# Seven half-size products for the last matrix product of a retention and gated-MLP kernel

## Chip, cores and metric

The kernel runs on one core of a Trainium2 chip. The metric is device time in microseconds of one execution; below, the median of three runs. TensorE does the matrix products, DVE (VectorE), ACT (ScalarE) and POOL (GpSimd) work element by element, and all data moves by DMA issued from SP's queue.

## What is computed

```python
scores = scale * q @ k.T * gamma[h] ** (i - j)   # causal, 8 heads of 64, 576 positions, 8 batches
x = (scores @ v)  ->  (batch, 576, 512)
h = relu(x @ w_in)                               # 512 -> 1024
u, v = h[..., :512], h[..., 512:]
v_n = (v - mean(v)) / sqrt(var(v) + 1e-6)
v_s = w_spatial @ v_n + b_spatial                # over the 576 positions
out = (u * v_s) @ w_out                          # 512 -> 512
```

## The kernel before

Retention is computed in four chunks of 128 positions and a tail of 64, with a state carried from chunk to chunk, on 64x64 matmuls. The rest are matmuls of 128 rows by 128 columns of weights with 256, 288 or 512 moving columns. Each fp32 operand is kept as two parts, an upper one in the matmul's number format (`hi`, an ACT copy that rounds) and the rest (`lo`, a subtraction); a product of two such operands is three matmuls, hi*hi, hi*lo and lo*hi (`mm3`). So before an operand can be used, ACT has to round it and DVE or POOL to subtract.

The order of every instruction on every engine is written out by hand in two tables. `ORDER` covers the weights and batches 0 and 1, and the start of batch 2. `STEADY` is run six times, for batches a = 2 to 7, with b = a + 1 and c = a + 2 for what is already started of the next ones; names with a batch past 7 are left out. A name stands for a chain (a generator), and each time that it occurs its next step is issued. Each engine and the DMA queue runs its instructions in the order in which the tables issue them, and waits for its data. `BANKS` names, in the same order, the one of four PSUM banks that each larger product uses. The names that matter here:

- `d.b.c`, `T.b`: loads of chunk c and of the tail of batch b. `k`, `q`: scaling of a chunk's keys and queries.
- `g` scores and mask, `p` state update, `b` the burst of products of a chunk and its evacuation (steps: carried products, `turned`, carried products, values, evacuation), `t` the tail's scores and mask, `e` its evacuation.
- `R`, `K`: for batches 2 to 7, the input x (kept in fp32 in `x32`) is cut in quarters; `R` splits three quarters as they are (`plain_quarter`), and `K` forms four differences of quarters and splits them (`summed_quarter`): a subtraction, an ACT cast, a subtraction. The letters at the end of a name (`p`, `v`) choose POOL or DVE for the first and last of them.
- `W.b.kind.m.i`: product i of seven (Strassen's scheme, in Winograd's form) of x and w_in, kind 0 for the v half and kind 1 for the u half, for output half m; each is six matmuls and then one to two additions into `u`. `A.s.step` makes the weights' combinations for it.
- `v`: relu and normalization. `X.b.t.db`: `w_spatial` times v_n, then the gate with u, then the split of the result into hi and lo in a `slot` (`g_chain`).
- `F.b.t.mb`: the product of the gated result and w_out, 12 matmuls for each of eight output blocks, an ACT copy to a tile `o0` to `o3`, and its DMA out (`f_chain`).

There are two `slot` tiles of two parts by four 128-row blocks by 576 columns. For batches 2 to 7 the seven right factors of x lie in seven quarters of the two slots, and the split gated product takes all of slot 1; so `K`, which writes quarters of slot 1, can only follow `F` of the batch before.

Of the kernel before, what the change touches and what calls it, by code (L numbers as in the profile page):

```python
# [10 lines left out]
F32 = mybir.dt.float32  # L11
# [35 lines left out]
    p.0.1.vv v.0.0 p.0.1.vv k.0.2.p b.0.1 w.0.0.vp b.0.1 q.0.2.p w.0.0.vp g.0.2 b.0.1 w.0.1.pp w.0.1.pp b.0.1
    p.0.2.pp T.0 p.0.1.vv d.0.3 w.0.2.pp p.0.2.pp v.0.0 b.0.1 v.0.0 g.0.2 w.0.1.pp p.0.2.pp w.0.1.pp b.0.2 p.0.2.pp
    b.0.2 c.t w.0.2.pp p.0.2.pp v.0.1 v.0.1 t.0.p t.0.p w.0.1.pp k.0.3.v b.0.2 b.0.2 d.1.0 w.0.2.pp q.0.3.p g.0.3
    t.0.p p.0.3.pp v.0.1 p.0.3.pp v.0.0 v.0.1 p.0.3.pp b.0.2 b.0.2 v.0.2 g.0.3 S d.1.0 p.0.3.pp d.1.1 b.0.3 m  # L50
    w.0.0.vp b.0.3 d.1.1 v.0.1 g.1.0 b.0.3 b.0.3 k.1.0.p w.0.2.pp S v.0.2 v.0.2 d.1.0 v.0.0 D.2.1 q.1.0.p s.0.p
    g.1.0 e.0.p v.0.0 S v.0.1 p.1.0.vv S e.0.p w.0.2.pp v.0.1 b.0.3 v.0.0 e.0.p S v.0.2 v.0.4 v.0.0 v.0.4 k.1.1.p
    p.1.0.vv v.0.2 d.1.2 s.2.p v.0.4 v.0.1 b.0.3 v.0.0 q.1.1.p v.0.1 w.0.0.vp s.1.v v.0.2 v.0.4 d.1.1 p.1.0.vv v.0.3
    s.2.p v.0.3 v.0.1 s.0.p v.0.2 w.0.2.pp s.4.p v.0.3 U.1 v.0.3 v.0.4 p.1.0.vv s.5.v d.1.2 b.1.0 T.1 U.1 s.3.v
    g.1.1 p.1.1.pp s.1.v v.0.2 v.0.4 p.1.0.vv b.1.0 s.4.p b.1.0 s.5.v k.1.2.p s.3.v v.0.2 v.0.2 b.1.0 p.1.1.pp D.0.3
    v.0.4 U.0 b.1.0 p.1.1.pp b.1.0 v.0.3 v.0.4 v.1.0 w.0.2.pp v.0.3 d.1.2 U.0 g.1.1 w.0.1.pp w.0.1.pp v.1.0 v.1.0
# [868 lines left out]
```

## Time and profile before

| | |
|---|---|
| median of three runs | 528.0 us (527.73 to 528.03) |
| the profiled execution | 528.6 us, span 526.7 us |
| TensorE busy | 499.3 us (95%), 7376 matmuls |
| DVE, POOL, ACT busy | 353.3 us (67%), 236.6 us (45%), 222.0 us (42%) |
| granted TensorE clock | 0.996 of full speed |
| one pass of STEADY | 61.12 us |

The span runs from the first to the last instruction. In the lists of instructions, each line has the start in us, the duration in us, the engine, the operation, "out<-in" by the program's tile names (numbers left out: `m` is a PSUM bank of the larger products, `r` a PSUM tile of retention, `x` is `x32`), the shape, the count, and in square brackets the idle time of the engine before it with what ended it. Rows of windows give start and end, the length, then busy time and count of PE, PEld (weight loads), DVE, ACT and POOL, then granted clock, share of the DMA engines in use and GB/s. Rows of groups give busy time, mean ns of one, and the idle time before them by releaser. All lines bear the number 155, that of the helper which records every operation, so the tiles tell them apart.

### The profile page before, as it was taken

To read this page: it belongs to the slowest core of one execution; us is meant where nothing else is said; L and a number is where in the kernel's file an instruction comes from. 1 tells how busy PE (TensorE), PEld (TensorE's weight loads), DVE (VectorE), ACT (ScalarE), POOL (GpSimd) and SP (SyncE) were. 2 spreads that over 40 slices of the span, in tenths; PEclk is the share of its full clock that TensorE was granted. 3 is DMA by queue.
4 is the path that set the end of the run, shared out by engine and by line. 5 is a ranking of instruction groups with operands and counts; after the bars stand their busy time and mean duration, and the time that the engine had idled before them with its cause. 6 is when DMAs were issued, how large, how long until landed. Compare 5 with 4: busy or idle time off the path is not lost.

```text
span 526.7 us, 17043 instructions
## 1 busy us (share of the span) xinstructions
PE 499.3 (95%) x7376; PEld 475.8 (90%) x7376; DVE 353.3 (67%) x803; ACT 222.0 (42%) x502; POOL 236.6 (45%) x216
## 2 busy tenths in 40 slices
PE   0789999999998999999999999999999999999897
PEld 0668998799998999999999999999999999998896
DVE  4998888961536884579654995569745895538640
ACT  4347535562152452444344451445434452444422
POOL 2887769411156720667027740557216750444000
PEclk9999999999998999999999999999999999999999
DMA  8995342403315430163202650155201600020002
GB/s 289 410 321 187 116 157 82 123 18 101 113 59 170 144 105 2 46 197 126 78 2 94 182 168 4 42 157 160 87 2 52 221 11 2 1 91 1 0 1 91
DMA packets 29948, 55.53 MB, mean 105 GB/s; under 512 B 3249, under 2 KB 15793, under 8 KB 29618
## 3 DMA queue, kind: packets, MB, share of 16 engines
q1 hardware_dynamic: 29874, 54.45, 31.4%
q8 instruction: 58, 0.95, 0.7%
q14 instruction: 16, 0.13, 0.1%
HBM read 45.00 MB, written 9.44 MB: 103 GB/s over the span
## 4 chain that ended last, share of the span: by engine, by line
PE 80%; DVE 9%; POOL 3%; issue 3%; DMA 2%; ACT 2%; SPq 0%; ACTq 0%; POOLq 0%; DVEq 0%
PE m L155 69%; PE r L155 11%; DVE u L155 3%; DMA lent_slot<-in_w_in 1%; POOL x L155 1%; DVE sm L155 1%; DMA kn<-in_qkv 1%; POOL u L155 1%; DVE m L155 1%; DVE s L155 1%; DVE vn L155 1%; DVE slot L155 1%; SPq L155 0%; ACT vt L155 0%; DVE dec L155 0%
## 5 line engine op out<-in xcount | busy, mean ns | idle before, releaser
L155 PE MATMUL m<-wsp,vn 128*128 128x288 f32 x768 | 113.5, 297 | 0.4 <-DVE vt L155 0.3
L155 PEld LDWEIGHTS m<-wsp,vn 128*128 128x128 f32 x768 | 105.2, 188 | 2.0 <-DVE vt L155 1.3
L155 PE MATMUL m<-slot,wout 128*128 128x288 f32 x768 | 104.1, 294 | 0.2 <-DVE f L155 0.2
L155 PEld LDWEIGHTS m<-slot,wout 128*128 128x128 f32 x768 | 102.3, 188 | 0.7 <-issue 0.6
L155 PE MATMUL m<-slot,win 128*128 128x288 f32 x480 | 74.2, 299 | 1.8 <-ACT u L155 1.0
L155 DVE TENSOR_TENSOR u<-m,u 128x256 f32<-128x256 f32 (+1 forms) x144 | 59.0, 431 | 24.5 <-ACT u L155 16.5
L155 PEld LDWEIGHTS m<-slot,win 128*128 128x128 f32 x480 | 66.7, 188 | 5.9 <-ACT u L155 2.6
L155 PE MATMUL m<-win,slot 128*128 128x256 f32 (+1 forms) x312 | 56.5, 325 | 2.7 <-issue 1.8
L155 POOL TENSOR_TENSOR x<-x 128x576 f32<-128x576 f32 (+1 forms) x28 | 42.7, 1524 | 21.1 <-DVE slot L155 13.0
L155 PEld LDWEIGHTS m<-win,slot 128*128 128x128 f32 x312 | 45.1, 193 | 7.9 <-DVE u L155 2.1
L155 DVE TENSOR_TENSOR slot<-m,slot 128x288 fp32r<-128x288 f32 x56 | 25.3, 455 | 36.6 <-ACT slot L155 35.8
L155 ACT COPY o<-m 128x288 f32<-128x288 f32 x64 | 25.4, 400 | 55.7 <-PE m L155 52.7
L155 ACT COPY u<-m 128x288 f32<-128x288 f32 (+1 forms) x54 | 20.8, 385 | 57.0 <-PE m L155 42.1
L155 ACT CAST slot<-m 128x288 fp32r<-128x288 f32 x56 | 21.7, 404 | 52.2 <-DVE m L155 52.1
L155 DVE TENSOR_TENSOR slot<-x,slot 128x576 fp32r<-128x576 f32 x24 | 26.9, 1123 | 22.3 <-ACT slot L155 22.3
L155 POOL TENSOR_TENSOR x<-xt 128x256 f32<-128x256 f32 x6 | 4.4, 738 | 81.6 <-DVE xt L155 81.6
L155 PE MATMUL m<-quarter,slot 128*128 128x256 f32 x288 | 39.0, 285 | 2.0 <-ACT o L155 1.3
L155 PEld LDWEIGHTS m<-quarter,slot 128*128 128x128 f32 x288 | 36.2, 191 | 2.8 <-ACT o L155 1.5
L155 DVE SCALAR_TENSOR_TENSOR m<-u,m 128x288 f32<-128x288 f32 x48 | 20.9, 456 | 25.1 <-PE m L155 25.1
L155 ACT CAST slot<-x 128x576 fp32r<-128x576 f32 x42 | 28.4, 680 | 17.0 <-POOL x L155 14.3
L155 POOL TENSOR_SCALAR u<-u 128x512 f32<-128x512 f32 x18 | 26.7, 1500 | 17.6 <-DVE u L155 15.0
L155 POOL TENSOR_TENSOR slot<-x,slot 128x576 fp32r<-128x576 f32 x18 | 26.1, 1465 | 18.2 <-ACT slot L155 18.2
(128 smaller groups left out, 917.2 us busy)
## 6 DMA issues: line engine op xcount, KB each, us to landing
qk<-in_qkv SPq DMA_DIRECT2D x30, 512.0 KB, 4.4
out<-o SPq DMA_DIRECT2D x64, 144.0 KB, 1.8
kn<-in_qkv SPq DMA_DIRECT2D x30, 256.0 KB, 5.1
vv<-in_qkv SPq DMA_DIRECT2D x30, 256.0 KB, 5.4
tail<-in_tails SPq DMA_DIRECT2D x8, 384.0 KB, 3.4
lent_slot<-in_w_in SPq DMA_DIRECT2D x4, 512.0 KB, 7.2
raw<-in_w_in SPq DMA_DIRECT2D x4, 512.0 KB, 6.2
raw<-in_w_out SPq DMA_DIRECT2D x4, 512.0 KB, 6.5
```

The source lines that it names most:

```text
L155: ins = op(*args, **kw)
```

## The change

The product with w_out is made by seven half-size products for batches 2 to 7 too: `W` gets a kind 2, with the seven factors of w_out made by `A.2` (18 steps in ORDER), and the gated product is no longer split in `g_chain` but written to `u` in fp32, cut in quarters and split by `r` (as `R`) and `J` (as `K`). Its seven right factors lie in the same quarters of both slots as those of x. A product of kind 2 is six matmuls of 288 columns; results are added up in four tiles `o` and a quarter of `u`, and the DMA out is the last step of products 2, 5, 4 and 3. In STEADY all of `J` is `vp`: the difference on DVE, the last subtraction on POOL.

To make room, the operand of the tail (`xt`) shares a buffer with the tail's load, so that `T.b` follows the tail products of the batch before; the tail's queries are scaled in place, after its scores; a scratch tile of the tail's normalization lies in `o`. The tail's mask is no longer loaded: the mask of the chunks is used, in two operations of 64 partitions each. ORDER, STEADY and BANKS are written anew as a whole.

```diff
     def made(s, k):
+        if (s, k) == (2, 1):
+            return [slot(0)[:, i, 0:2, HALF:HALF + 256] for i in range(2)]
+        if (s, k) == (2, 2):
+            return [keep(f"quarter22{i}", [P, 2, 256], F32R, tag=f"f{2 + i}") for i in range(2)]
...
     def g_of_batch(b):
         if b not in gs:
-            gs[b] = slot(b if b < PLAIN else 1)
+            gs[b] = slot(b)
...
     def mask_tail(b):
         a = keep("att", [P, 2, 2, TL])
-        ve.tensor_tensor(out=a, in0=ot, in1=amt, op=ALU.mult)
+        for r in range(2):
+            ve.tensor_tensor(out=a[half[r]], in0=ot[half[r]], in1=am[half[r], :, 2 * r:2 * r + 2], op=ALU.mult)
...
     # g_chain
-        if b < PLAIN:
-            ve.tensor_tensor(out=ps, in0=ps, in1=u_tile_of()[:, db, ts], op=ALU.mult)
-        else:
-            ve.scalar_tensor_tensor(out=ps, in0=u_tile_of()[:, db, ts], scalar=0.0, in1=ps, op0=ALU.max, op1=ALU.mult)
+        u = u_tile_of()[:, db, ts]
+        if b >= PLAIN:
+            ve.scalar_tensor_tensor(out=u, in0=u, scalar=0.0, in1=ps, op0=ALU.max, op1=ALU.mult)
+            yield
+            return
+        ve.tensor_tensor(out=ps, in0=ps, in1=u, op=ALU.mult)
...
     # product_chain
-        else:
+        elif kind == 1:
             c11, c12, c21, c22 = u[:, m, lo], u[:, m, hi], u[:, 2 + m, lo], u[:, 2 + m, hi]
+        else:
+            o = results()
+            c11, c21, c12, c22 = (o[:, 0], o[:, 3], o[:, 2], o[:, 1]) if m == 0 else (u[:, 0, lo], o[:, 0], o[:, 1], o[:, 2])
...
+        if kind == 2 and i in (2, 5, 4, 3):
+            t, mb, src = {2: (0, m, c11), 5: (1, 2 + m, c22), 4: (0, 2 + m, c21), 3: (1, m, c12)}[i]
+            dma(out[b, mb * P:(mb + 1) * P, t * HALF:(t + 1) * HALF], src)
+            yield
...
+        "r": lambda b, k, m, how: plain_quarter(u_tile_of, int(k), int(m), on(how)),
+        "J": lambda b, n, how: summed_quarter(u_tile_of, int(n), on(how[0]), on(how[1])),
```

The part of the new STEADY from the first X of a batch to its end:

```
X.a.0.0 X.a.1.2 d.c.0 W.a.1.1.4 X.a.0.1 b.b.2 X.a.1.3 t.b.v d.c.1 p.b.3.vp d.c.0
X.a.0.1 X.a.0.0 b.b.2 X.a.1.1 X.a.1.2 X.a.1.3 X.a.1.0 t.b.v g.b.3 q.c.0.p X.a.0.2 r.a.0.0.p r.a.1.1.v X.a.1.1
X.a.1.0 r.a.0.0.p d.c.0 p.b.3.vp J.a.5.vp X.a.0.2 p.b.3.vp X.a.0.3 r.a.1.1.v J.a.7.vp J.a.6.vp W.a.2.0.1 X.a.0.3
W.a.2.1.1 J.a.5.vp J.a.6.vp J.a.5.vp b.b.3 J.a.6.vp r.a.1.0.v b.b.3 g.c.0 W.a.2.1.1 W.a.2.0.1 b.b.3 J.a.7.vp
b.b.3 r.a.1.0.v k.c.0.p W.a.2.0.6 J.a.7.vp W.a.2.0.2.v J.a.4.vp e.b.p J.a.4.vp e.b.p W.a.2.0.7 W.a.2.0.6
J.a.4.vp e.b.p W.a.2.0.5 W.a.2.0.2.v W.a.2.0.4 R.b.0.0.p W.a.2.0.2.v W.a.2.0.2.v W.a.2.0.7 W.a.2.0.5 W.a.2.0.4
W.a.2.0.3 W.a.2.1.3 W.a.2.0.5 p.c.0.vv W.a.2.0.3 W.a.2.0.5 b.b.3 R.b.1.1.v g.c.0 R.b.0.0.p p.c.0.vv W.a.2.1.6
W.a.2.1.2.v K.b.5.pv W.a.2.1.7 W.a.2.0.4 R.b.1.1.v W.a.2.1.6 R.b.1.0.p W.a.2.1.2.v K.b.7.pv p.c.0.vv W.a.2.1.7
W.a.2.1.5 W.a.2.1.2.v p.c.0.vv K.b.7.pv W.a.2.1.4 W.a.2.1.2.v W.a.2.1.5 W.a.2.1.4 K.b.5.pv K.b.6.pv R.b.1.0.p
K.b.6.pv d.c.1 K.b.4.pp K.b.4.pp W.a.2.1.5 K.b.6.pv K.b.4.pp W.a.2.1.3 K.b.7.pv W.a.2.1.4 W.a.2.0.3 W.a.2.1.3
K.b.5.pv p.c.0.vv W.a.2.1.5
```

More of the change, by code (lines that the diff above doesn't have):

```diff
@@ L47 @@
[L47 to L56, printed above, removed]
@@ L110, in retention_gmlp @@
 @with_exitstack
-def retention_gmlp(ctx, tc, qkv, tails, w_in, w_sp, b_sp, w_out, amask, tmask, qscale, kdec, sdec, out):
+def retention_gmlp(ctx, tc, qkv, tails, w_in, w_sp, b_sp, w_out, amask, qscale, kdec, sdec, out):
     nc = tc.nc
@@ L218, in load_tail @@
     def load_tail(b):
-        t = keep("tail", [P, 3, NP * TL])
+        t = cp.tile([P, 3, NP * TL], F32, name=f"tail{b}", tag="tail")
         dma(t, tails[b])
@@ L225, in weight_of_out, with results @@
         return keep(f"wout{i}", [P, NDB, DM], F32R)
+    def results():
+        return keep("o", [P, NMB, HALF])
     def normed(i):
@@ L276, in summed_quarter @@
         yield
+    late = 9, 10, 11, 16, 17
     def made_weight(s, step, eng=po):
-        t = [x32()[:, k, :512].rearrange("p (a n) -> p a n", a=2) for k in range(4)]
+        t = [(u_tile_of() if s == 2 and step in late else x32())[:, k, :512].rearrange("p (a n) -> p a n", a=2) for k in range(4)]
         if s == 1:
@@ L302, in made_weight @@
          lambda: both(held, t[2], t[0], ALU.subtract), lambda: upper(3, held), lambda: lower(3, held),
-         lambda: whole(t[2], 1, 0), lambda: both(t[2], t[2], t[3], ALU.subtract), lambda: upper(4, t[2]), lambda: lower(4, t[2])][step]()
+         lambda: whole(t[2], 1, 0), lambda: both(t[2], t[2], t[3], ALU.subtract), lambda: upper(4, t[2]), lambda: lower(4, t[2])]
+        if s == 2:
+            steps[9] = lambda: whole(t[1], 0, 1)
+            steps += [lambda: whole(held, 0, 0), lambda: both(held, held, t[1], ALU.subtract)]
+        steps[step]()
         yield
@@ L402, in prep_tail @@
     def prep_tail(b, eng=po):
-        t = keep("qsct", [P, NP, TL])
-        eng.tensor_tensor(out=t, in0=tail[b][0], in1=qs, op=ALU.mult)
+        t = tail[b][0]
+        eng.tensor_tensor(out=t, in0=t, in1=qs, op=ALU.mult)
         scaled[b, NC] = t
@@ L494, in evac_lo, with xt_of @@
         ve.tensor_tensor(out=lo, in0=o, in1=hi.bitcast(F32), op=ALU.subtract)
+    def xt_of(b):
+        if b not in xts:
+            t = cp.tile([P, 3 * NP * TL], F32R, name=f"xt{b}", tag="tail")
+            xts[b] = t[:, :2 * NCB * TL].rearrange("p (a i n) -> p a i n", a=NCB, i=2)
+        return xts[b]
     def place_tail(b, eng=po):
+        xt = xt_of(b)
         halves = [xt[:, :, i].rearrange("q a (t n) -> q a t n", t=2) for i in range(2)]
@@ L629, in v_chain @@
                 for i in range(2):
-                    pe.matmul(pf, xt[:, cb], win[i][:, cb, DH:], start=(cb == 0 and i == 0), stop=(cb == NCB - 1 and i == 1))
+                    pe.matmul(pf, xt_of(b)[:, cb], win[i][:, cb, DH:], start=(cb == 0 and i == 0), stop=(cb == NCB - 1 and i == 1))
             yield
@@ L743, in f_chain @@
         ts = slice(t * HALF, (t + 1) * HALF)
-        o = keep(f"o{mb}", [P, HALF])
+        o = results()[:, mb]
         ps = bank()[:, :HALF]
```

158 lines of the change are left out of this document (83 added, 75 removed).

## The prediction

> **What bounds the kernel now.** I read the page's busy totals and chain first, then a table of windows cut at the first product of each batch, then the instructions of one steady batch in order of time.
>
> ```profile
> span 526.7 us, 17043 instructions
> PE 499.3 (95%) x7376; PEld 475.8 (90%) x7376; DVE 353.3 (67%) x803; ACT 222.0 (42%) x502; POOL 236.6 (45%) x216
> ...
> PE 80%; DVE 9%; POOL 3%; issue 3%; DMA 2%; ACT 2%; SPq 0%; ACTq 0%; POOLq 0%; DVEq 0%
> ```
>
> TensorE is busy 95% of the span and carries 80% of the chain that ended last. No other engine is above 67%.
>
> ```profile
> 0.00:40.00 40.00, 23.04 (x641) 18.48 (x641) 32.40 (x65) 16.00 (x32) 26.56 (x30) 1.00 0.93 338
> ...
> 120.00:163.35 43.35, 41.36 (x689) 40.24 (x687) 17.81 (x34) 14.28 (x36) 14.40 (x13) 1.00 0.27 84
> ...
> 287.34:348.46 61.12, 60.70 (x930) 58.99 (x929) 41.78 (x99) 25.53 (x60) 28.40 (x28) 1.00 0.31 97
> ...
> 470.80:526.70 55.90, 50.33 (x367) 48.08 (x366) 28.77 (x78) 17.88 (x41) 7.64 (x7) 0.99 0.08 27
> 326.70:334.20 7.50, 7.50 (x61) 7.50 (x57) 3.44 (x9) 3.69 (x9) 1.35 (x2) 1.00 0.01 2
> 334.20:348.46 14.26, 14.26 (x112) 14.26 (x111) 6.85 (x11) 6.84 (x16) 9.48 (x8) 1.00 0.19 64
> 287.34:308.93 21.59, 21.54 (x372) 20.36 (x373) 19.75 (x51) 8.84 (x21) 15.89 (x17) 1.00 0.59 180
> ```
>
> The columns are window, length, then busy time of TensorE, its weight loads, DVE, ACT and POOL. A steady batch lasts 61.12 us, and TensorE is idle for 0.42 of it: there only fewer TensorE instructions, or a new wait, can move the time. TensorE's other idle time lies in the first 40 us (17.0, loading), before batch 2 (2.0) and in the last batch (5.6). The last three rows are parts of a steady batch: the last four X, the stage of F, and the W and v stage at its start. Beside F, DVE works 6.85 us of 14.26 and POOL 9.48, so the work that prepares the next batch (R, K) has room there.
>
> **What the change removes from TensorE.**
>
> ```profile
> 324.16 0.27 PE L155 MATMUL r<-qsc,sh 64*64 64x64 f32 x1
> 325.03 0.65 PE L155 MATMUL r<-vv,kn 64*64 64x64 f32 x32
> 326.65 1.85 PE L155 MATMUL m<-wsp,vn 128*128 128x288 f32 x12
> 328.61 1.75 PE L155 MATMUL m<-wsp,vn 128*128 128x288 f32 x12
> 330.48 1.76 PE L155 MATMUL m<-wsp,vn 128*128 128x288 f32 x12
> 334.20 12.82 PE L155 MATMUL m<-slot,wout 128*128 128x288 f32 x96
> 346.86 0.87 PE L155 MATMUL m<-quarter,slot 128*128 128x256 f32 x6
> ```
>
> F is 96 matmuls in 12.66 us (334.20 to 346.86), 0.132 us each. Seven products of two output halves with six matmuls make 84: 12 fewer, 1.59 us a batch, 9.5 us in six batches. With the 0.42 of idle, a steady batch could come down to 59.1 us.
>
> **What it adds on the other engines, per batch 2 to 7.**
>
> ```profile
> L155 DVE TENSOR_TENSOR slot<-m,slot 128x288 fp32r<-128x288 f32 x56 | 25.3, 455 | 36.6 <-ACT slot L155 35.8
> L155 ACT CAST slot<-m 128x288 fp32r<-128x288 f32 x56 | 21.7, 404 | 52.2 <-DVE m L155 52.1 <-issue 0.2
> L155 DVE TENSOR_TENSOR u<-m,u 128x288 f32<-128x288 f32 x72 | 31.0, 446 | 2.7 <-PE m L155 1.9 <-POOL u L155 0.3
> L155 ACT CAST slot<-x 128x576 fp32r<-128x576 f32 x42 | 28.4, 680 | 17.0 <-POOL x L155 14.3 <-PE m L155 2.8
> L155 ACT COPY o<-m 128x288 f32<-128x288 f32 x64 | 25.4, 400 | 55.7 <-PE m L155 52.7 <-ACT slot L155 3.0
> ```
>
> Gone are the eight ACT casts and eight DVE subtractions of the split of each g_chain (404 and 455 ns; the gate itself stays, now into u) and the eight ACT copies of F's results. Added are 7 ACT casts of 576 columns (680 ns), 4 ACT copies, 4 DVE and 7 more subtractions that make the right factors (r: 1 POOL, 2 DVE; J: 4 DVE before the cast, 4 POOL after), 12 DVE accumulations of 288 columns (446 ns) and 2 DVE additions. ACT comes out even: 8 x 0.40 + 8 x 0.40 = 6.4 us gone, 7 x 0.68 + 4 x 0.39 = 6.3 added. DVE loses 3.6 and gains some 6 x 0.67 + 12 x 0.45 + 2 x 0.33 = 10.1; POOL gains 5 x 1.43 = 7.2. Averaged over the batch this fits (41.8 + 6.5 of 59 on DVE, 28.4 + 7.2 on POOL). But it all falls behind the last X, where before TensorE had twelve microseconds of F ready.
>
> **The resource that decides.**
>
> ```profile
> 329.09 0.73 POOL L155 TENSOR_TENSOR x<-xt 128x256 f32<-128x256 f32 x1 [14.16 <-DVE xt L155]
> 330.68 0.46 DVE L155 SCALAR_TENSOR_TENSOR m<-u,m 128x288 f32<-128x288 f32 x1 [1.73 <-PE m L155]
> 334.83 0.75 DVE L155 TENSOR_TENSOR slot<-x,slot 128x576 fp32r<-128x576 f32 x1
> 335.50 0.82 DVE L155 SCALAR_TENSOR_TENSOR m<-u,m 128x288 f32<-128x288 f32 x2
> 338.63 1.43 POOL L155 TENSOR_TENSOR slot<-x,slot 128x576 fp32r<-128x576 f32 x1
> 338.68 1.99 DVE L155 TENSOR_TENSOR slot<-x,slot 128x576 fp32r<-128x576 f32 x1
> 340.14 1.83 POOL L155 TENSOR_TENSOR x<-x 128x576 f32<-128x576 f32 x1
> 237.87 1.07 POOL L155 TENSOR_TENSOR kn<-kn,kd 128x512 f32<-128x512 f32 x1
> 238.88 2.96 POOL L155 TENSOR_SCALAR u<-u 128x512 f32<-128x512 f32 x2
> 239.41 0.74 DVE L155 SCALAR_TENSOR_TENSOR vn<-u,sm,vn 128x512 fp32r<-128x512 f32 x1
> ```
>
> A DVE subtraction of 576 columns whose two inputs lie in SBUF ran in 0.67 us (334.83, the next one starting at 335.50). Issued at 338.68, just after a POOL subtraction of the same kind had started (338.63, 1.43 us), it took 1.99 and ended 0.61 after POOL's; the next POOL one, issued at 340.14, took 1.83 and ended 1.30 after DVE's. So such operations of the two engines run one after the other. By the Trainium skill, "SBUF — State Buffer", section "Who interferes with whom", DVE and GpSimd share a port pair under an exclusive lock; these rows agree. The page would also have any SBUF-reading POOL operation take part, and there the trace differs: a DVE operation with two SBUF inputs took its usual 0.74 us at 239.41, inside a single-input POOL one. In the stage at issue POOL has two-input operations only, so page and trace give the same sum there, the forecast's; were there no lock, the sum would be that of the first rival.
>
> **The stage walked through.** Clock t from the first X of a steady batch; every start on TensorE in STEADY's written order. Eight X at 1.87 (328.61 to 330.48) and the value products of chunk 2 (about 0.5): 15.5. Two products i=1 (0.79 each): 17.1. Scores and last burst of the next batch: 2.0 (324.16 to 326.65, less 0.46 for the update from 325.03): 19.1. Twelve more products and an update: 29.1. Scores and the first carried product: 29.9. There W.0.0.2 of the next batch is due, which needs the lower half of R.1.0, a POOL operation behind a long queue. What must go through the shared resource before it: J.5's subtraction can start when the sixth X is out (11.7), passed to DVE 0.2 later (the second X from 328.61 has its gate at 330.68), gated (0.4), and one decay done: t = 12.7. From there, on DVE the four J subtractions, the lower halves of r.1.1, r.1.0 and R.1.1 (7 x 0.67 = 4.7), two additions and a decay (scaled by columns from 0.67: 1.0); on POOL the four lower halves of J, R.0.0, R.1.0 and K's first three subtractions (9 x 1.43 = 12.9), kn (1.07) and x<-xt (0.73). Sum 20.4. Packed without a gap that ends at 33.1, less some 0.8 by the shorter second operation of a pair (0.61 for 0.67, 1.30 for 1.43): 32.2, so TensorE waits 2.3 us. Three times nothing can run until ACT has made the upper half (0.68 each, J.5, J.6, R.0.0): 35.1, wait 5.2. I take the middle, 3.7, for wait and order alike are read from rows and neither end is nearer. What TensorE sees of it comes in pieces: the second carried product of chunk 3 behind `turned`, which ACT reaches after the upper half of r.1.0; W.2.0.7 behind J.7's lower half; W.0.0.2.
>
> STEADY's first part, W and v, is rewritten too. Counted at their row means, DVE's operations ahead of the first X sum to 27.6 us after and 29.1 before, so I charge no new wait there; 0.5 us a batch more or less is covered by the range.
>
> So a steady batch is 59.1 + 3.7 = 62.8, 1.7 more than now; between 61.4 (+0.3) and 64.3 (+3.2). Five batches are followed by another: +8.5, between +1.5 and +16.
>
> **The last batch.**
>
> ```profile
> 495.07 1.86 PE L155 MATMUL m<-wsp,vn 128*128 128x288 f32 x12 [0.27 <-DVE vt L155]
> 510.05 12.82 PE L155 MATMUL m<-slot,wout 128*128 128x288 f32 x96
> 522.96 0.40 ACT L155 COPY o<-m 128x288 f32<-128x288 f32 x1 [1.22 <-PE m L155]
> ```
>
> From its first X (495.07) to the span's end are 31.6 us, F being ready when the last X is done. After the change nothing of a next batch covers the J chain. By the same walk: last X out at 14.9, two products 16.5, J.6's lower half at 18.7, J.7's at 21.4 (TensorE waits 2.2 and 1.1), then the rest of the products to 29.5, three DVE accumulations behind the last, 1.4, and the 3.34 us that lie between the last ACT copy's end (523.36) and the end of the span: 34.3, or 2.7 more. Without the lock the same chain gives about 32.8, 1.2 more. I take +2.0.
>
> **The smaller edits.**
>
> ```profile
> L155 DVE TENSOR_TENSOR att<-r,amt x8: 391/408/415, 31.0 to 436.8; 128x256 f32<-128x256 f32 x8
> amt<-in_tmask SPq DMA_DIRECT2D x1, 128.0 KB, 9.9
> tail<-in_tails SPq DMA_DIRECT2D x8, 384.0 KB, 3.4
> L155 POOL TENSOR_TENSOR x<-win,win 128x512 f32<-128x512 f32 x3 | 3.9, 1291 | 3.5 <-DVE f L155 2.1 <-DVE x L155 1.4
> 10.00:15.00 5.00, 2.04 (x64) 1.86 (x64) 4.93 (x9) 1.80 (x3) 4.45 (x4) 1.00 1.06 398
> ```
>
> The tail mask in two steps is one more DVE operation a batch, 0.4 us if each half is charged the 408 ns of the whole; it lies where DVE waits for X: 0, at most 0.4 a batch. The mask's own load of 128 KB goes: at 398 GB/s, the pace of the loading phase in the row above, 0.3 us, if anything waits for it: 0 to -0.3. T.b moves behind the tail products of the batch before, whose operand shares its buffer; it lands in 3.4 us and the tail scores come some 5 us later: 0, and a wait of up to 3.4 if the two loads queued with it on SP hold it up. The weights of w_out need 18 more steps in ORDER, 14 of them element by element on 512 columns (8 on POOL at 1.29 us, 6 on DVE at about half): 14 us over two engines that were busy 17.8 and 14.4 of the 43.4 us before batch 2: 0, but five of these lie in the last stretch with R and K of batch 2, where TensorE already waits 2.0: at worst 3. The new ORDER as a whole: the loads, and the DVE work ahead of each product of batches 0 and 1, come in another sequence but to nearly the same sums, so 0, -3 to +3. The output's eight stores a batch stay; the loads of the next chunks queue behind some of them on SP and are wanted 8 us later: 0.
>
> Sum: +8.5 + 2.0 = +10.5. The profiled execution took 528.6 us (span 526.7), 0.6 above the median of 528.0; I put the sum on the median: 538.5, rounded to 538. The likeliest case's own range is 530 to 546.
>
> **The rivals.** *The engines do not hold each other up* (a gain). Then POOL's queue alone is the limit: J.6's cast ends at 17.3, and eight subtractions of 1.43, kn, x<-xt and one cast (0.7) end R.1.0 at 31.2. The wait is 1.3, the batch 60.4, five times -0.7, the last batch +1.2: -2.3, 525.7. For it: POOL is idle for 4.8 us of each F stage now, and most of DVE's operations read PSUM and are never held up. Against it: the rows at 338.6. *Everything is hidden* by an order that I misjudge: 6 x -1.59 and +1.0 for the accumulations after the last product: -8.5, 519.5. For it: in the present order DVE is busy 19.75 of 21.59 us of the first stage and TensorE still loses nothing; such an order can be found. Against it: the port sum of 20.4 us is there in any order of those steps. The point from which it decides is a wait of 2.0 us a batch. *The products are not fewer* can be excluded: the loop issues 84.
>
> **How the numbers follow.** From no change a measurement of this kernel tells about 0.2%, 1 us. The forecast holds 0.60 (0.55 of it slower, 0.05 where the packed bound and the smaller edits meet zero), the POOL queue alone 0.22 (0.18 faster, 0.02 same, 0.02 slower), all hidden 0.18 (0.17 faster, 0.01 same). That is 0.35 faster, 0.08 same, 0.57 slower. The range must reach to the hidden case: 520 to 545 leaves out half of that case and the far end of the walk, together 2 in 10.
>
> **What would show it.** 696 matmuls with wout or its quarters in place of 768; a steady batch near 62.8 us with some 4 us of idle TensorE in two or three places: ahead of r<-qsc,sh, of a product with J.7, and of the first products of the next batch, released by POOL slot. DVE subtractions x<-x of 1.2 us and more on the mean in place of 0.67. Near 59.5 us and no such idle time, the walk is wrong; if the loss lies before batch 2, ORDER is what I mis-sized.

## The result: 5.0% slower

The changed kernel takes 555.0 us (median of six runs, 553.4 to 557.5), the kernel before, in runs on the same chip, 528.1. The ratio is 1.0505, with a 95% interval of 1.0476 to 1.0533. The forecast of 538 had the right sign, but 555 lies above its range of 520 to 545. The profiled execution took 553.4 us with a span of 551.6, at a granted clock of 1.000; everything below compares spans, 526.7 and 551.6.

From the page of the changed kernel, its span and the busy totals:

```profile
span 551.6 us, 17110 instructions
PE 503.2 (91%) x7304; PEld 469.8 (85%) x7304; DVE 423.6 (77%) x886; ACT 226.2 (41%) x476; POOL 304.0 (55%) x257
```

72 matmuls are gone, as computed, yet TensorE's busy time rises from 499.3 to 503.2 us, and it is now idle for 9% of the span instead of 5%. DVE is busy 70.3 us more, POOL 67.4. To see where, here are windows of the changed kernel: one batch from its first X (326.69) to the next batch's first X (391.56), cut at the next batch's first W (361.40), and the last batch to the end of the span.

```profile
326.69:361.40 34.71, 31.74 (x435) 30.21 (x428) 23.41 (x42) 11.54 (x22) 18.57 (x13) 1.00 0.21 71
361.40:391.56 30.16, 29.89 (x493) 27.78 (x489) 28.28 (x73) 14.35 (x32) 19.60 (x19) 1.00 0.37 114
326.69:391.56 64.87, 61.63 (x924) 57.99 (x917) 51.70 (x113) 25.89 (x54) 38.18 (x31) 1.00 0.28 91
516.25:551.60 35.35, 27.26 (x198) 26.11 (x196) 19.26 (x31) 6.22 (x12) 7.22 (x5) 1.00 0.10 34
```

The same cuts of the kernel before:

```profile
316.63:347.00 30.37, 30.37 (x372) 30.14 (x371) 15.67 (x31) 10.92 (x26) 9.40 (x8) 1.00 0.07 24
347.00:377.86 30.86, 30.33 (x562) 28.76 (x560) 26.47 (x68) 14.74 (x33) 19.00 (x18) 1.00 0.54 167
316.63:377.86 61.23, 60.70 (x931) 58.90 (x929) 42.14 (x99) 25.66 (x59) 28.39 (x26) 1.00 0.31 96
495.07:526.70 31.63, 27.80 (x208) 27.57 (x208) 8.51 (x20) 6.00 (x16) 0.00 (x0) 0.99 0.11 38
```

I call the first part of a batch (X, the product with w_out, up to the next first W) the first stretch, the rest (W, v) the second. The loss of a batch shows in the first stretch: 30.37 to 34.71, while the second even falls, 30.86 to 30.16. The fall of the second is work that moved: more of retention's small products (scores, carried products and values) now stand ahead of W, so the first stretch has 435 matmuls instead of 372, and its weight loads take as long as before (30.14 and 30.21 us) although the product with w_out is shorter. What is new in it is idle time. I read TensorE's waits from the weight loads: they were idle for 2.33 us of the batch before (61.23 - 58.90) and are for 6.88 now (64.87 - 57.99). By the matmul rows, whose ends the profile models, the idle time rises from 0.53 to 3.24 us and the busy time by 0.93.

The span's 24.9 us are made up of three parts, taken from the starts of the first X of each batch. The part before batch 2 ends at 196.63 instead of 194.65, +2.0. From there to the first X of the last batch are 319.62 us (196.63 to 516.25) instead of 300.42, +19.2, or 3.8 a pass. The last batch takes 35.35 instead of 31.63, +3.7.

Now the first stretch instruction by instruction, from the list of the changed kernel in order of time (engines PEld, DVE, ACT and POOL, parts left out):

```profile
341.24 1.43 POOL L159 TENSOR_TENSOR slot<-u,slot 128x576 fp32r<-128x576 f32 x1 [3.60 <-ACT slot L159]
341.56 1.72 DVE L159 TENSOR_TENSOR slot<-u,slot 128x576 fp32r<-128x576 f32 x1
343.21 1.54 DVE L159 TENSOR_TENSOR u<-u 128x576 f32<-128x576 f32 x2
...
344.78 1.25 ACT L159 CAST slot<-u 128x576 fp32r<-128x576 f32 x2 [3.61 <-DVE u L159]
345.53 1.41 POOL L159 TENSOR_TENSOR slot<-u,slot 128x576 fp32r<-128x576 f32 x1 [2.86 <-ACT slot L159]
346.06 1.50 DVE L159 TENSOR_TENSOR slot<-u,slot 128x576 fp32r<-128x576 f32 x1 [0.95 <-ACT slot L159]
346.90 1.56 POOL L159 TENSOR_TENSOR kn<-kn,kd 128x512 f32<-128x512 f32 x1
347.59 1.48 DVE L159 TENSOR_TENSOR u<-u 128x576 f32<-128x576 f32 x1
348.43 3.52 POOL L159 TENSOR_TENSOR slot<-u,slot 128x576 fp32r<-128x576 f32 x2
...
359.80 1.62 POOL L159 TENSOR_TENSOR slot<-x,slot 128x576 fp32r<-128x576 f32 x1
...
346.13 0.13 PEld L159 LDWEIGHTS r<-qsc,st 64*64 64x64 f32 x1 [1.04 <-ACT r L159]
350.40 0.70 PEld L159 LDWEIGHTS m<-slot,wout 128*128 128x128 f32 x5 [1.31 <-POOL slot L159]
358.98 0.83 PEld L159 LDWEIGHTS m<-slot,wout 128*128 128x128 f32 x6 [0.68 <-DVE o L159]
360.56 0.59 PEld L159 LDWEIGHTS r<-qk 64*64 64x64 f32 x32 [0.75 <-ACT slot L159]
...
361.44 0.66 PEld L159 LDWEIGHTS m<-win,slot 128*128 128x128 f32 x5
```

Follow the two engines in alternation: POOL starts a lower half at 341.24, and DVE's, started 0.3 later, takes 1.72 us where 0.75 is its time alone; it ends at 343.28, 0.61 after POOL's. At 345.53 and 346.06 the same; there POOL's next operation (kn) then takes 1.56 instead of some 1.05, behind DVE, and DVE's next 1.48 behind kn. J.7's lower half waits behind kn and is the first of the pair at 348.43; TensorE, which needs it, resumes at 350.40. The four idle times in brackets of the weight loads are all the waits for another engine in this stretch, 3.78 us. In the list of waits of the weight loads from 196.63 on:

```profile
PEld m L159 <- POOL slot L159: 11.0, 9, 2.0
PEld r L159 <- ACT r L159: 5.6, 5, 1.5
...
PEld r L159 <- DVE st L159: 4.3, 3, 1.4
```

The columns are total us, how often, and the longest. The first row is mostly J's, the second `turned`, which ACT reaches behind the cast of r.1.0; the third is the last wait ahead of W in batches 2, 3 and 5. The durations (min, median, max in ns) from batch 2 on, of POOL's lower halves of r and J, of DVE's of R and K, of DVE's of r, and of DVE's J differences:

```profile
L159 POOL TENSOR_TENSOR slot<-u,slot x30: 1401/1463/1926, 206.0 to 538.7; 128x576 fp32r<-128x576 f32 x30
L159 DVE TENSOR_TENSOR slot<-x,slot x20: 744/1426/1921, 225.8 to 493.5; 128x576 fp32r<-128x576 f32 x20
L159 DVE TENSOR_TENSOR slot<-u,slot x12: 1483/1609/1912, 211.5 to 534.5; 128x576 fp32r<-128x576 f32 x12
L159 DVE TENSOR_TENSOR u<-u x24: 744/758/1872, 209.6 to 536.1; 128x576 f32<-128x576 f32 x24
```

None of DVE's lower halves of r (third row) ran at 0.75 us: the quickest of twelve took 1.48. Of J's differences (last row) half did.

### The profile page after: what moved, and what is told of

Its sections match the earlier page's. It is cut to its first block, busy times and chain, and to the rows that moved or that the text cites. A ratio compares the mean times of both kernels' runs of the same rounds, so it can differ in the third digit from the quotient of the medians.

```text
span 551.6 us, 17110 instructions
## 1 busy us (share of the span) xinstructions
PE 503.2 (91%) x7304; PEld 469.8 (85%) x7304; DVE 423.6 (77%) x886; ACT 226.2 (41%) x476; POOL 304.0 (55%) x257
## 5 line engine op out<-in xcount | busy, mean ns | idle before, releaser
L159 POOL TENSOR_TENSOR slot<-u,slot 128x576 fp32r<-128x576 f32 x32 | 49.6, 1556 | 74.7 <-ACT slot L159 74.7
L159 PE MATMUL m<-slot,wout 128*128 128x288 f32 x480 | 71.3, 297 | 6.5 <-POOL slot L159 6.0
L159 PEld LDWEIGHTS m<-slot,wout 128*128 128x128 f32 x480 | 65.8, 188 | 8.7 <-POOL slot L159 7.7
L159 PE MATMUL m<-slot,quarter 128*128 128x288 f32 x360 | 57.3, 300 | 2.6 <-ACT slot L159 1.1
L159 ACT CAST slot<-u 128x576 fp32r<-128x576 f32 x46 | 30.3, 671 | 62.8 <-DVE u L159 62.5
L159 PEld LDWEIGHTS m<-slot,quarter 128*128 128x128 f32 x360 | 50.0, 188 | 5.7 <-ACT slot L159 1.3
L159 POOL TENSOR_TENSOR qsc<-qk,qs 128x512 f32<-128x512 f32 (+1 forms) x26 | 30.5, 1174 | 31.5 <-DMA qk<-in_qkv 30.4
L159 ACT CAST slot<-x 128x576 fp32r<-128x576 f32 (+1 forms) x43 | 28.2, 672 | 37.4 <-POOL x L159 29.6
L159 POOL TENSOR_TENSOR u<-u 128x256 f32<-128x256 f32 (+2 forms) x25 | 21.7, 869 | 36.8 <-ACT u L159 23.5
L159 DVE TENSOR_TENSOR slot<-x,slot 128x576 fp32r<-128x576 f32 (+1 forms) x26 | 34.8, 1363 | 1.2 <-ACT slot L159 1.2
L159 DVE TENSOR_TENSOR o<-m,o 128x288 f32<-128x288 f32 x66 | 28.8, 452 | 8.9 <-PE m L159 7.2
```

The source lines that it names most:

```text
L159: ins = op(*args, **kw)
```

## The experiments

The theory is the prediction's: two-input SBUF operations of DVE and POOL exclude each other, and the lower halves of J, r and R are late by that. The expectations name the rivals that each run is to tell apart. All runs in one table; the stretches are of batches 2 to 5 (medians, us), "last" from the last batch's first X to the end of the span, "start" the first X of batch 2. The ratio is to runs of the kernel before on the same chip.

| kernel | us | ratio, 95% interval | first | second | last | start |
|---|---|---|---|---|---|---|
| before | 528.1 | | 30.3 | 30.8 | 31.6 | 194.7 |
| changed | 555.0 | 1.0505, 1.0476 to 1.0533 | 34.7 | 30.2 | 35.4 | 196.6 |
| e1 DVE one input | 534.9 | 1.0112, 1.0078 to 1.0147 | 32.3 | 29.4 | 33.0 | 196.6 |
| e2 J on DVE | 538.3 | 1.0176, 1.0140 to 1.0213 | 32.8 | 29.9 | 32.7 | 196.4 |
| e3 turned early | 554.2 | 1.0477, 1.0441 to 1.0514 | 34.7 | 30.2 | 35.3 | 197.4 |
| e4 before, mask in two steps | 529.4 | 1.0005, 0.9992 to 1.0019 | 30.3 | 30.8 | 31.6 | 195.1 |
| e5 more on DVE | 549.0 | 1.0397, 1.0366 to 1.0427 | 33.0 | 31.2 | 32.7 | 198.1 |
| e6 all on DVE | 547.5 | 1.0367, 1.0335 to 1.0399 | 32.9 | 31.3 | 32.7 | 198.2 |
| e7 J on POOL | 565.7 | one run | 37.0 | 30.2 | 36.8 | 196.1 |
| e8 R earlier | 556.2 | 1.0540, 1.0511 to 1.0570 | 35.4 | 31.0 | 32.7 | 196.8 |
| e9 one input, step 0 | 534.9 | 1.0104, 1.0046 to 1.0162 | 32.6 | 29.4 | 33.0 | 195.2 |
| e10 J on DVE, decay on POOL | 536.7 | 1.0143, 1.0095 to 1.0191 | 31.6 | 30.3 | 32.7 | 197.0 |
| e11 short A.2 | 553.8 | one run | 34.7 | 30.2 | 35.3 | 196.4 |
| e12 second input in PSUM | 565.2 | 1.0689, 1.0628 to 1.0750 | 36.6 | 31.7 | 32.8 | 201.2 |
| e13 other split | 546.8 | 1.0346, 1.0299 to 1.0393 | 31.7 | 32.2 | 32.7 | 198.5 |
| e14 POOL one input | 559.8 | 1.0575, 1.0527 to 1.0623 | 32.8 | 32.8 | 35.0 | 200.1 |
| e15 the same, sums excepted | 558.8 | 1.0535, 1.0504 to 1.0566 | 32.8 | 32.8 | 34.9 | 198.6 |
| e16 POOL one input, r and J alone | 550.7 | 1.0425, 1.0392 to 1.0457 | 34.1 | 30.2 | 34.0 | 197.8 |

**Moving J (e2, e7).** In STEADY, every J of the changed kernel is `vp`.

```diff
-J.a.5.vp ... J.a.6.vp ... J.a.7.vp ... J.a.4.vp
+J.a.5.vv ... J.a.6.vv ... J.a.7.vv ... J.a.4.vv     (e2)
+J.a.5.pp ... J.a.6.pp ... J.a.7.pp ... J.a.4.pp     (e7)
```

> The changed kernel, with the last subtraction of the four J on DVE in place of POOL. Theory: the sum of the excluded operations ahead of R.1.0's lower half falls by 4 x 0.76 = 3.0 us and two of the three casts stay uncovered, so the stage goes from 34.75 to 32 to 33 and the total to 540 to 546. Rival B (DVE's own queue is the limit: it is busy 51.7 of 65 us): DVE gets 2.7 us more work where it is late already, the stage stays or grows, total 555 to 565.

> The changed kernel with J's four differences on POOL as well as its last subtractions. Theory: the excluded sum grows by 4 x 0.76 = 3.0 us, the stage from 34.7 to 36.5 to 38, the total to 564 to 575. Rival B (DVE's queue was the limit): DVE is relieved by 2.7 us and more of waiting, the stage falls to 33 or less, total under 548.

With J's last step on DVE the first stretch is 32.8 us, with all of J on POOL 37.0. e2 came out 2 us under the interval that was expected, e7 within it. The waits on POOL's slots, of e2 and then of e7:

```profile
PEld m L159 <- POOL slot L159: 0.9, 1, 0.9
```
```profile
PEld m L159 <- POOL slot L159: 16.8, 16, 2.4
```

0.9, 11.0 and 16.8 us of such waits go with 32.8, 34.7 and 37.0 us of first stretch: J's last step on POOL makes 1.9 us of the loss of a first stretch, and 16.7 us of the time. e2's 32.8 is still 2.5 us above the 30.3 of before, and it doesn't say by itself whether J is late there by mutual exclusion or by the mere length of POOL's operations (1.40 us alone for DVE's 0.75).

**One input on DVE (e1, e9).** DVE's subtractions of r, J, R and K and its additions into the sums become one-input operations (e9: the subtractions alone, reading one column over and over).

```diff
+    def two(eng, out, a, b, op, only):
+        if eng is ve:
+            eng.tensor_scalar(out=out, in0=only, scalar1=0.0, scalar2=None, op0=ALU.add)
+        else:
+            eng.tensor_tensor(out=out, in0=a, in1=b, op=op)
-        e2.tensor_tensor(out=lo, in0=t, in1=hi.bitcast(F32), op=ALU.subtract)
+        two(e2, lo, t, hi.bitcast(F32), ALU.subtract, hi.bitcast(F32))
```

> The changed kernel, but DVE's subtractions of r, J, R and K and its additions of kind 2 read one SBUF input in place of two (same size, same order, same waits on ACT; the results lose the second term). Theory (two-input operations of DVE and POOL exclude each other): DVE and POOL no longer stop each other in the stage, first X to first W.0 of the next batch falls from 34.75 us to 31 to 32, a pass of STEADY from 65.0 to about 62, the total from 555 to 536 to 541. Rival A (the length of POOL's queue and the chain of dependences alone): DVE's operations take 0.67 us either way, so the stage stays at 34.5 to 35 and the total at 553 to 557.

> The changed kernel, but DVE's subtractions of r, J, R and K read one SBUF input with a step of 0 (one element of each row, read 288 times), in place of two inputs; the results lose what is not read. The first run with one input had operations of 0.44 us when alone, and POOL still held them up to 1.2 us, so it did not separate the causes. Theory: at step 0 they take 0.6 to 0.7 us, as two inputs do when alone, and POOL no longer holds them up: DVE's median for them falls from 1.4 to 1.6 us to under 0.75, the stage from 34.7 to 31.5 to 32.5, the total from 555 to 534 to 541. Rival D (the shorter operations made the gain of the first run, not the absence of blocking): stage 34 and more, total 549 to 556.

Both took 534.9 us, but neither tested what it was to test. DVE's lower halves in e1, and one of them beside POOL in order of time:

```profile
L159 DVE TENSOR_SCALAR slot<-slot x32: 442/1160/1687, 211.5 to 517.1; 128x576 fp32r<-128x576 f32 x32
```
```profile
334.29 1.43 POOL L159 TENSOR_TENSOR slot<-u,slot 128x576 fp32r<-128x576 f32 x1 [3.31 <-ACT slot L159]
334.91 1.12 DVE L159 TENSOR_SCALAR slot<-slot 128x576 fp32r<-128x576 f32 x1
```

Alone such an operation takes 0.44 us, not 0.75; beside POOL it is still held, to 0.31 us after POOL's end. e9's are the same (0.444 us the quickest, 1.20 the median), so e9's time lies in its theory's interval for another reason than the one expected. The operations got shorter and the exclusion stayed, and the 20 us that were won can't be given to either. By the Trainium skill, "SBUF — State Buffer", section "Who interferes with whom", `tensor_scalar` on DVE can enter a mode that uses the port pair shared with GpSimd, and then contends with it. The rows agree, with 0.44 us and 1.12.

**Second input in PSUM (e12).** The operation and its length stay, the second operand is a zero in PSUM.

```diff
+    zero = bo[:, 0:1, 400:401]
+    ve.memset(zero, 0.0)
...
+            eng.tensor_tensor(out=out, in0=only, in1=zero.broadcast_to([P, 2, HALF]), op=op)
```

> The changed kernel, but each of VectorE's subtractions for r, J, R and K keeps its operation, its length and its place in the order, and only its second input is taken from a zero in PSUM instead of from SBUF, so that the second term of these differences is left out of the results. VectorE's operations are then as long as in the changed kernel when alone (some 0.75 us for 128x512), but no longer read two SBUF inputs. Theory (the mutual exclusion of two-input SBUF operations of VectorE and GpSimd is what delays the first half of a batch): medians stay at 0.75 us, means fall from 1.4-1.6 us to under 1.0, the stretch from first X to the next batch's first W falls from 34.7 us to 31 to 32.5, and the time to 532 to 541 us. Rival D (the one-input runs gained only because their operations were shorter, 0.44 us for 0.75): the stretch stays at 34 us or over and the time at 549 to 556 us.

```profile
L159 DVE TENSOR_TENSOR slot<-slot,r x30: 741/744/757, 216.0 to 508.1; 128x576 fp32r<-128x576 f32 x30
```

The durations say what the theory says: not one of the 30 operations took over 0.757 us. For this operation of DVE's it is the second SBUF input that makes the two engines exclude each other. The time says nothing on its price: the zero lies in a PSUM bank that TensorE writes for retention, and the scheduling then has DVE wait for TensorE and TensorE for DVE:

```profile
PEld r L159 <- DVE slot L159: 12.3, 4, 3.1
```

The granted clock was 0.972 in this run, too. Both parties of the expectation missed its 565 us.

**One input on POOL (e14, e15, e16).** The mirror of it, without a new wait: POOL's subtractions read one tensor, and one element per partition of the other. The instructions, their order and their waits are the changed kernel's, and DVE's side is untouched.

```diff
+    def two(eng, out, a, b, op):
+        if eng is po:
+            eng.tensor_scalar(out=out, in0=a, scalar1=b[:, 0, 0:1] if len(b.shape) > 2 else b[:, 0:1], scalar2=None, op0=op)
+        else:
+            eng.tensor_tensor(out=out, in0=a, in1=b, op=op)
-            eng.tensor_tensor(out=c11, in0=c22, in1=c11, op=ALU.add)
+            two(eng, c11, c22, c11, ALU.add)      (e14 alone)
+        if eng is po and whole is u_tile_of:      (e16: r and J alone)
```

> The mirror of the one-input runs, on GpSimd's side: the changed kernel, but each of GpSimd's subtractions for r, J, R and K, and its additions into the sums of products, reads one tensor, and takes its second operand from one element per partition of the same tile, so that the results lose the rest of the second term. Every instruction, its place in the order and its waits stay; VectorE's instructions are untouched. GpSimd's operation gets no shorter: its one-input operation on 128x512 takes 1.5 us in the changed kernel, its two-input one on 128x576 1.4 us. Theory (it is the exclusion between two-input SBUF operations of the two engines): VectorE's subtractions fall from means of 1.0 to 1.6 us to under 1.0 us though they were not touched, the stretch from first X to the next batch's first W falls from 34.7 us to 31.0 to 33.3, and the time to 533 to 546 us. Rival D (the one-input runs gained because the operations were shorter, and the delay is the mere length of the queues): the stretch stays at 34 us or over and the time at 549 to 558 us.

> As the run with GpSimd's operations at one input, but the additions into the sums of products (2.04 us with one input, 1.56 with two) are the changed kernel's again, so that only the subtractions of r, J, R and K on GpSimd read one tensor. Theory (with two-input operations against each other gone in the first half, the loss there goes): the first stretch stays at 32.7 us (34.7 in the changed kernel), although each of these GpSimd operations is 0.3 us longer, the second returns from 32.8 to 30.2 to 31.2, and the time falls to 538 to 547 us. Rival (the longer second stretch comes from R's longer operations, or VectorE's freed time gives nothing in the end): the second stretch stays at 32 us or over and the time at 549 to 560 us.

> As the run before it, but GpSimd's one-input operations only for the lower parts of r and J (30 in batches 2 to 7, all in the first stretch); K and R have their two-input operations again. The results lose the rest of the second term of r and J alone. Theory (the exclusion delays r and J; the longer second stretch of the last two runs came from the one-input operations for K, 3.4 to 5.5 us in a row): the first stretch stays at 32.0 to 33.2 us, the second comes back to 30.2 to 31.0, and the time falls to 541 to 549 us. Rival (VectorE freed early only moves the wait to the second stretch): the second stays at 32 us or over and the time at 551 to 560 us.

Durations in e14, of POOL's lower halves and of the three groups of DVE:

```profile
L159 POOL TENSOR_SCALAR slot<-u,slot x27: 1716/1724/1916, 209.5 to 537.6; 128x576 fp32r<-128x576 f32 x27
L159 DVE TENSOR_TENSOR slot<-x,slot x20: 749/756/1226, 228.6 to 497.2; 128x576 fp32r<-128x576 f32 x20
L159 DVE TENSOR_TENSOR slot<-u,slot x11: 835/1039/1235, 214.9 to 537.7; 128x576 fp32r<-128x576 f32 x11
L159 DVE TENSOR_TENSOR u<-u x23: 746/757/759, 213.1 to 539.6; 128x576 f32<-128x576 f32 x23
```

DVE's medians fall from 1.43 to 0.76 and from 1.61 to 1.04 us though nothing of DVE was changed and POOL's operations became 0.3 us longer. The first stretch falls by 2.0 us, to 32.8, within the theory's bounds: ahead of W, the wait for `turned` falls from 1.0 to 0.4 us, and the 1.4 us of waits just ahead of W are gone; the decay and the addition that stand in DVE's queue there, 1.29 and 1.31 us in the changed kernel, take 0.41 and 0.45 in e15. J.7's wait stays at 1.3. The times miss both intervals in e14, and e15 does what its rival said (second stretch 32 or over, 549 to 560 us): the second stretch rises by as much or more, because K's one-input operations now stand in a row on POOL, and the first W product after them waits. The granted clock was 0.977 and 0.980, but in a batch at 1.00 (from 331.58 in e14) the second stretch is still 32.65 us. POOL and the weight loads of e15:

```profile
358.03 5.46 POOL L159 TENSOR_SCALAR x<-x 128x576 f32<-128x576 f32 x3
363.47 1.72 POOL L159 TENSOR_SCALAR slot<-x,slot 128x576 fp32r<-128x576 f32 x1
```
```profile
365.25 1.23 PEld L159 LDWEIGHTS m<-win,slot 128*128 128x128 f32 x10 [2.09 <-POOL slot L159]
```

In the changed kernel the three took 4.90 us. The second row is the lower half of R.1.0. It ends 35.1 us after the first X (330.10), in the changed kernel 34.7: W's first two loads don't need it and start early, the third waits 2.09 us. So the cut at W's first load flatters e14 and e15, whose operand for W comes no earlier. I had put the longer second stretch down to the additions into the sums, and e15 put those back: no stretch moved by over 0.1 us, so the addition was not it. e16 put K and R back, and the second stretch was 30.2 again. But its first fell by only 0.6 us, to 34.1, where 32.0 to 33.2 were expected. Its DVE runs free beside r and J, yet J.7's lower half still stands behind kn on POOL and each of J's is 0.3 us longer, so TensorE's wait for it stays, 1.26 us where it was 1.31:

```profile
346.50 1.35 POOL L159 TENSOR_TENSOR kn<-kn,kd 128x512 f32<-128x512 f32 x1
347.83 3.42 POOL L159 TENSOR_SCALAR slot<-u,slot 128x576 fp32r<-128x576 f32 x2
```
```profile
349.61 0.70 PEld L159 LDWEIGHTS m<-slot,wout 128*128 128x128 f32 x5 [1.26 <-POOL slot L159]
```

Its 550.7 us lie just above the theory's 541 to 549 and below the rival's 551 to 560: neither is confirmed by it.

**`turned` (e3).** It is moved ahead of r.1.0's cast on ACT, where TensorE waited 5.6 us in all for `ACT r`.

```diff
-J.a.5.vp b.b.3 J.a.6.vp r.a.1.0.v b.b.3 g.c.0
+J.a.5.vp b.b.3 b.b.3 J.a.6.vp r.a.1.0.v g.c.0
```

> The changed kernel, with the one-element ACT copy that the second carried product of chunk 3 waits for issued ahead of the ACT upper half of r.1.0. Theory: the wait ahead of that product shrinks by about 1 us but the first products of the next batch are due when R.1.0's lower half is ready, so the wait comes back there: total 553 to 556, unchanged. Rival C (each wait that TensorE shows adds to the time by itself): 5 x 1.0 us less, total 549 to 550.

The wait for `ACT r` fell from 5.6 to 2.8 us in all, and no stretch changed: what is won ahead of J.7's lower half is lost at it. In the first stretch from 327.38 us the first wait is 0.46 us instead of 1.04, J.7's 1.78 instead of 1.31.

**More on DVE (e5, e6, e8).** e5 is e2 and e3 with all of r and R on DVE and one step of K's; e6 puts all of K there too; e8 is e5 with the last step of R.1.0 ten names earlier.

```diff
-r.a.0.0.p ... R.b.0.0.p ... R.b.1.0.p ... K.b.4.pp
+r.a.0.0.v ... R.b.0.0.v ... R.b.1.0.v ... K.b.4.pv     (e5)
+K.b.4.vv ... K.b.5.vv ... K.b.6.vv ... K.b.7.vv        (e6)
-p.c.0.vv W.a.2.1.7 ... K.b.5.pv K.b.6.pv R.b.1.0.v   (e8, against e5)
+p.c.0.vv W.a.2.1.7 R.b.1.0.v ... K.b.5.pv K.b.6.pv
```

> The changed kernel with J's last subtraction, all of r and R and the last of K.4 on DVE, and the one-element copy ahead of r.1.0's cast; only kn, qsc, x<-xt and K's four differences stay on POOL. Theory: of the excluded operations ahead of R.1.0 three more go from 1.43 to 0.67 us against the run with J alone on DVE (stage 32.8 us): stage 30.5 to 31.5, a pass of STEADY 60 to 61, total 525 to 531. Rival B (DVE's queue is the limit by now): the stage stays at 32.5 to 34, total 538 to 545.

> As the run before it, and K's four differences on DVE too. Theory: the excluded sum falls by 3 us more, but K's differences ran on POOL beside DVE's accumulations, which read PSUM and exclude nothing, so little of that is gained and DVE's queue grows by 2.7 us: total within 4 us of the run before it, either way. Rival A (POOL's queue alone made the waits): all of POOL's queue ahead of R.1.0 is gone, stage at 30 us, total 521 to 524.

> As the first run of this group, with the lower half of R.1.0, which the first product of the next batch needs, issued on DVE some nine instructions earlier. Theory: if that operation still ends last, the stage falls by another 0.5 to 1 us, total 2 to 5 us under the first run; if other waits end last by now (a bank, the differences of K), nothing changes (within 1 us).

e5 missed its 525 to 531 by 18 us, and the rival's 538 to 545 by 4: DVE becomes the late one. It is busy 52.86 us of the 64 from 196 to 260 us (POOL 25.04), and the weight loads wait for DVE's slots and `o`:

```profile
PEld m L159 <- DVE slot L159: 8.5, 14, 1.2
...
PEld m L159 <- DVE o L159: 4.3, 9, 0.7
```

e6 stays within 2 us of it. e8 lost 7 us more, where 2 to 5 were to be won: the wait for the state that DVE updates, `r <- DVE st`, rises from 4.5 to 10.1 us (the granted clock fell too, from 0.991 to 0.978).

**Splits between (e10, e13).** e10 is e2 with the decays of one chunk a batch on POOL; e13 moves three kinds of step more.

```diff
-p.c.0.vv
+p.c.0.pp                                   (e10 and e13)
-v.a.0.v ... k.b.1.v ... K.b.5.pv
+v.a.0.p ... k.b.1.p ... K.b.5.vv           (e13)
```

> The changed kernel with the last subtraction of the four J on DVE, and the two decays of chunk 0 of the next batch but one on POOL. With J on DVE, the decay was held up to 1.56 us behind a difference of K on POOL, and two accumulations and the last product behind it in DVE's queue. Theory: TensorE's wait of 1.0 us ahead of the last product shrinks to 0.3, total 538 to 533 to 536. Rival: POOL's queue, which gets 1.2 us more, ends last by now: 538 to 542.

> The version with J on VectorE and one decay step on GpSimd (536.7 us), with three more steps moved: one u addition and one one-input step of K from VectorE to GpSimd, and one two-input step of K from GpSimd to VectorE. Theory (a batch pays for every change of turn between the two engines' two-input operations, so that one engine should hold them and the other the one-input work): 533 to 537 us, the first stretch at 31.0 to 31.6 us. Rival (GpSimd's own queue grows longer than it can hide): 537 to 543 us.

e10, 536.7 us, is the best version with the whole computation, still 1.4% above the time before (0.95 to 1.91%). One of its batches, and its waits for another engine in the first stretch of that batch (to 352.23 us):

```profile
320.66:382.57 61.91, 61.17 (x922) 57.82 (x916) 50.97 (x115) 25.69 (x54) 33.11 (x29) 1.00 0.30 95
```
```profile
PEld r L159 <- ACT slot L159: 0.5, 1, 0.5
```

The waits of the changed kernel's first stretch are all but gone, and a batch still lasts longer than the 61.23 us before. e13 kept its first stretch (31.7 us), but the second went to 32.2 from 30.3: there `v.a.0` is on POOL, where such a one-input operation of 512 columns takes 1.59 us for DVE's 0.43 (means of the changed kernel), and TensorE waits 7.4 us for `DVE u` and 5.1 for `ACT u`. Its 546.8 us lie above both expectations.

**The start, and the mask (e4, e11).** e11 shortens A.2's operations on DVE and POOL to eight columns and makes its four subtractions ACT copies; e4 is the kernel before with its tail mask in two steps.

```diff
+            if s == 2:
+                out, a, b = (t[:, :, :8] for t in (out, a, b))                           (e11)
-        ve.tensor_tensor(out=a, in0=ot, in1=amt, op=ALU.mult)
+        for r in range(2):
+            ve.tensor_tensor(out=a[half[r]], in0=ot[half[r]], in1=amt[half[r]], op=ALU.mult)   (e4)
```

> The changed kernel with the work for the combinations of w_out all but taken out of DVE and POOL: 10 of the 14 operations on 8 columns per row in place of 256, the four subtractions replaced by ACT copies (the weights' values are then meaningless). Theory 1 (these operations delay the start of batch 2): the first X of batch 2, at 196.6 us, moves to 194 to 195, total 2 us less. Theory 2 (the new sequence of ORDER costs it): it stays at 196 to 197.

> The kernel before, with the tail's mask in two operations of 64 partitions. As predicted: nothing to measure, within 0.2% of 528. Rival: DVE is late at that place, each batch loses up to 0.4 us, 531.

Without A.2's work the first X of batch 2 starts at 196.36 us instead of 196.63. That is one run, and seven others with the same instructions up to there (e2, e3, e5 to e8, e10) range from 196.09 to 198.21, against 194.65 and 195.06 with the old ORDER. So no share of A.2 in the 2.0 us shows; that ORDER's new sequence makes them is what is left, and no run tests it by itself. The mask costs nothing that ten runs can show.

## Why the prediction came out too low

The forecast summed +8.5 for five passes, +2.0 for the last batch and 0 for the rest; the spans show +19.2, +3.7 and +2.0.

- **The mechanism held, but for one of three places.** TensorE is idle ahead of r<-qsc (1.04 us) and ahead of the product with J.7, released by POOL's slot (1.31), as the prediction said. It isn't idle at W: W's loads start at 361.44 as R.1.0's lower half ends (359.80 + 1.62). The third idle time lies before that, behind DVE's `o` and ACT's slot in this batch (0.68 and 0.75), behind DVE's `st` in batches 2, 3 and 5 (1.4). DVE's lower halves rose to means of 1.40 us (R, K) and 1.62 (r), J's differences only to 0.97, where 1.2 was to show it (the x<-x named there runs on POOL). e14 shows that this is the exclusion and not DVE's own load, and e12 that DVE's subtraction takes part in it by its two SBUF inputs.
- **The step that failed: "a steady batch could come down to 59.1 us".** That took 1.59 us for the 12 matmuls and 0.42 of idle time off each batch, some 10 us in five passes. The waits put on top were about as large as forecast: loads waited for another engine for 3.5 to 3.8 us in the first stretch of each of batches 2 to 6, 18.4 in all, where the sum has 5 x 3.7 = 18.5. Without them the five passes come to 301.2 us, and before they took 300.4: of the 10 us nothing came. In batch 4 the change of +3.64 is -0.91 of load time, +3.78 of waits in the first stretch, +0.3 of waits in the second (0.9 for 0.6) and +0.47 of other idle time. So the saving is 0.68 too large, and the idle time that was to go grew. The eleven rows of this batch's loads for the product with w_out, 5 to 12 loads each, sum to 11.65 us for 84, where one run of 96 took 12.72 before: 1.07 less, not 1.59. e10 shows the same from the other side: with 0.5 us of waits left in the first stretch, a batch takes 61.9 us.
- **"I take the middle, 3.7" was right in size, and partly by luck.** By the walk's clock R.1.0's lower half was to end at 33.6 (29.9 + 3.7), between 32.2 and 35.1; it ended at 34.7, near the late end (which leaves out the 0.8 us taken off the early one). The rows show why: POOL sat idle until a cast was done (2.86 us before 345.53), and both engines were held by each other's operations. That the waits still add up to 3.8 is because TensorE's own way to W took 30.9 us (34.7 - 3.8) instead of 29.9, and because a third wait that wasn't foreseen stands in for the one at W.
- **The last batch** had +2.0 between +1.2 and +2.7; +3.7 lies outside. TensorE waits 4.1 us there for J's operands, where the walk had 2.2 and 1.1. With J on DVE it is 32.7 us, 2.6 less: nothing of a next batch is there to be done while J's chain runs.
- **ORDER** was put at 0, between -3 and +3; TensorE has the same busy time (151.32 us) from 40 us to the first X of batch 2, in 156.63 us instead of 154.65. These are the sums of windows of the changed kernel and of before:

```profile
sum 156.63, PE 151.32 PEld 141.47 DVE 119.48 ACT 76.45 POOL 92.89; mean PE 50.44 PEld 47.16 DVE 39.83 ACT 25.48 POOL 30.96
```
```profile
sum 154.65, PE 151.32 PEld 142.21 DVE 111.72 ACT 73.94 POOL 79.53; mean PE 50.44 PEld 47.40 DVE 37.24 ACT 24.65 POOL 26.51
```

- **The smaller edits at 0:** the mask is right by e4, and A.2 as far as the one run e11 shows. **The rivals:** that POOL's queue alone decides (525.7) and that all is hidden (519.5) both fall. The range left out the walk's far end; with it, +16 for the passes, +2.7 and +3 give 550, still too little, for the walk's two ends vary the wait and not the 59.1.
- **What stays open.** How the 3.8 us of waits in the first stretch divide between the exclusion and the length of J's chain on POOL is not settled. Taking the exclusion away took 2.0 us of waits off it (e14, e15), but with operations 0.3 us longer the operand of W came no earlier, and for r and J alone it was 0.6 (e16); moving J's last step gave 1.9 (e2), which removes both. e1 shortened the operations as well, e12 added a wait. What the idle time of the loads that no engine's release ends consists of was not looked into. And no version tried brought the time to 528 us, so whether an order exists that turns the saved matmuls into a gain is open.

## What to carry to other kernels

Fewer matmuls are worth what their loads take in the new order, not their number times the mean of one long run: here 1.07 us for 1.59, and new gaps took most of that back. When work moves from the busiest engine to two others, sum what the two can't do at the same time, not each one's queue, and take the steps of a chain that hops between engines as uncovered unless you can name the work that fills each hop. A lower half that the next product waits for belongs on the engine that does it in the shorter time and with the least in front of it (J on DVE instead of POOL: 555.0 to 538.3 us); but each further step put there makes other things late (549.0). A test that takes contention away has to leave durations and waits as they were: look at both in its trace before you read its time.
